# Attention and two expert layers on one core: all three token-block pairs as seven block products

## The chip, the cores and the metric

The kernel runs on one core of a Trainium2 chip. Its time is the device time of one execution in microseconds (us); what is quoted is the median of three runs. An execution with the profiler on is read beside them. TensorE does the matrix products (PE in the profile, its weight loads PEld), VectorE (DVE), ScalarE (ACT) and GpSimd (POOL) the rest, SyncE (SP) starts most transfers. SBUF is the on-chip memory, PSUM the eight banks that TensorE writes.

## The reference

Three layers follow one another; each needs the whole output of the one before, token by token.

```python
def phi(x):                                   # linear attention, 4 batches x 8 heads x 576 tokens x 64
    proj = einsum('bhsd,df->bhsf', x, w_phi)  # 128 features
    proj = proj - max(abs(proj), axis=-1)
    return concatenate([exp(proj), exp(-proj)], axis=-1)
kv, z = einsum('bhsf,bhsd->bhfd', phi(k), v), sum(phi(k), axis=2)
attn = einsum('bhsf,bhfd->bhsd', phi(q), kv) / (einsum('bhsf,bhf->bhs', phi(q), z) + 1e-06)
# dense gated layer on x = attn as 2304 tokens x 512, hidden width 1536
g, val = x @ w_gate, x @ w_val
x2 = (g * sigmoid(g) * val) @ w_out
# routed layer: 8 experts, each token to the one with the largest logit
e = argmax(x2 @ w_gate2)
out = prob[e] * sigmoid(x2 @ w_output_gate)[e] * (relu(x2 @ w1[e]) @ w2[e])
```

The dense layer's weights arrive as 64-bit floating point numbers, all else as 32-bit ones.

## The kernel before

**Attention** goes in 16 units: one batch and two heads each. A unit has three chunks of `qk_mm` (TensorE), `qk_sub` (VectorE: a reduction and a subtraction over 768 numbers per partition) and `k_exp` (ScalarE), then `kv_mm`, the transposes of the query features `tq_mm` with their exponentials, `num_mm` in two halves, `normalise` (VectorE: three instructions) and the transposes `tx_mm`, whose result is cut into a high and a low part (`x_hi`, `x_lo`). Four units give the 512 features of the 576 tokens of one batch.

**Cutting in two.** A product of 32-bit accuracy is made of three faster ones: the operands are cut into a high part (a rounded copy, on ScalarE) and a low part (the rest, by a subtraction on VectorE or GpSimd), and TensorE adds high x high, high x low and low x high in PSUM. So every 128x128 piece of a weight costs three matmuls.

**Weight conversion.** 36 weight pieces of 128x512 are loaded as 64-bit numbers into three staging buffers and turned into 32-bit ones with integer arithmetic: `conv_scale` (ScalarE), `conv_round` (ScalarE or GpSimd), `conv_bits` (VectorE, two instructions) and `conv_add` (GpSimd).

**The dense layer** goes over six blocks of 384 tokens and, in each, over 12 slices of 128 hidden features. In blocks 0 to 3 a slice takes 12 matmuls for the gate, 12 for the value (`gv_mm`, 384 columns) and 9 for the output (`o_mm`, 512 columns), and its three weight pieces are cut anew in each block. Blocks 4 and 5 go together (`pair`): gate and value of both blocks form a 2x2 block product, computed with seven products instead of eight (Strassen's scheme in Winograd's form), each of 6 matmuls. That takes sums of the weights (`pair_split`, GpSimd) and of the operands (`x_sums`, VectorE). Block 4's output product runs along. The hidden values of block 5 are kept in place of weights that are done with, and a stretch behind the pair multiplies them by the output weights, 9 matmuls a slice.

**After a dense block** its output is copied and stored (`post_x2`), and small instructions turn it, make the logits and route the tokens (`post_log`, `post_mm`, `post_sum`, `route_a`, `route_b`).

**Order.** The attention of units 0 to 7, the conversion and block 0 are issued in the order of a table, `PLAN_TABLE`; `Plan.run` goes through it and puts `warmup` matmuls on TensorE where its own bookkeeping has a gap. Units 8 to 15 are spread over blocks 1 to 3 by `pace`. Each engine takes its instructions strictly in its own order, and so does SP with its transfers. Behind the dense layer comes the routed one (`quads`, `moe2`), fed by gathers from the stored rows `x2d`.

Of the kernel before, what the change touches and what calls it, by code (L numbers as in the profile page):

```python
# [19 lines left out]
P = 128  # L20
# [14 lines left out]
NSG = 25  # L35
BIG = float(1 << 20)
# [18 lines left out]
class Arena:  # L55
# [12 lines left out]
PLAN_TABLE = [0, 4, 2, 1, 13, 14, 5, 3, 16, 15, 30, 17, 19, 31, 22, 20, 11, 32, 18, 6, 7, 12, 46, 33, 34, 47, 21, 23,  # L68
# [30 lines left out]

class Plan:  # L100

    LAT = 20
    SINGLES = (7, 0, 3, 5, 1, 2, 6)
    PAIRS = (5, 0, 2, 1, 6)  # L110
# [1425 lines left out]
```

## Time and profile before

| | us |
|---|---|
| median of three runs | 886.86 (886.61 to 888.32) |
| profiled execution: its time | 885.83 |
| profiled execution: span, first to last instruction | 884.1 |
| TensorE busy | 864.3 (98%) |
| VectorE, ScalarE, GpSimd busy | 526.7, 474.6, 386.1 |

The span is what the profile shows between the first and the last instruction; 1.7 us of the execution lie around it. A matmul's listed duration runs from its start to its modelled end, and the next one starts before that; what a matmul costs in a full row is the distance between starts. Five places divide the span: 66.9 us (first matmul of the dense layer), 170 us (about the end of the planned part), 485.6 us (first block product of blocks 4-5), 604.7 us (start of the stretch behind them) and 636.7 us (the routed layer).

### The profile page before, as it was taken

How to read it: one execution, taken by the hardware profiler on the slowest of the kernel's cores; microseconds unless marked ns; L12 is line 12 of the kernel's file. 1: busy time of each engine (PE TensorE's matmuls, PEld its weight loads, DVE VectorE, ACT ScalarE, POOL GpSimd, SP SyncE). 2: the span in 40 equal slices, each digit the busy share in tenths (PEclk: the TensorE clock that was granted, in tenths of full speed). 3: DMA queues.
4: the chain of work that ended last, by engine and by line, in shares of the span. 5: the costliest groups of instructions: out<-in, count | busy, mean ns of one | idle time of the engine just before them, and what ended most of it. 6: DMA issues, size and time to landing. Idle time of an engine off the chain costs nothing. (4 is left out here: it accounts for less than half of the span.)

```text
span 884.1 us, 17277 instructions
## 1 busy us (share of the span) xinstructions
PE 864.3 (98%) x6846; PEld 752.7 (85%) x6848; DVE 526.7 (60%) x1028; ACT 474.6 (54%) x921; POOL 386.1 (44%) x339
## 2 busy tenths in 40 slices
PE   8989999999999999999999999999999999999995
PEld 5779989889998998888899999998778888888784
DVE  6999786543434645346647676676676444345693
ACT  5867876544444444453456655565433434344783
POOL 1676989445453434343446666546401112120120
PEclk9999999999999999999999999999999999999998
DMA  8766544110011111020000000005901233010650
GB/s 240 220 188 205 167 143 138 45 36 1 1 31 49 44 43 28 17 78 2 1 2 0 36 1 1 1 1 202 343 6 39 104 105 136 23 50 1 237 209 11
DMA packets 20362, 70.41 MB, mean 80 GB/s; under 512 B 5294, under 2 KB 5550, under 8 KB 18992
## 3 DMA queue, kind: packets, MB, share of 16 engines
q1 hardware_dynamic: 16704, 59.21, 20.7%
q0 software_dynamic: 3200, 9.48, 3.3%
q8 instruction: 55, 0.90, 0.4%
q10 hardware_dynamic: 368, 0.53, 0.2%
q14 instruction: 35, 0.29, 0.1%
HBM read 72.84 MB, written 10.00 MB: 94 GB/s over the span
## 5 line engine op out<-in xcount | busy, mean ns | idle before, releaser
L529 POOL TENSOR_TENSOR arena_r<-arena,arena_r 128x512 fp32r<-128x512 f32 x143 | 183.9, 1290 | 176.2 <-ACT arena_r L525 172.6
L525 ACT ACTIVATE arena_r<-arena 128x512 fp32r<-128x512 f32 x143 | 90.1, 631 | 156.8 <-PE banks L546 97.0
L545 PE MATMUL banks<-arena_r 128*128 128x384 f32 x384 | 135.0, 352 | 0.0
L547 PE MATMUL banks<-arena_r 128*128 128x384 f32 x384 | 129.2, 336 | 0.0
L546 PE MATMUL banks<-arena_r 128*128 128x384 f32 x384 | 129.2, 336 | 0.0
L1209 ACT ACTIVATE arena_r<-arena 128x512 fp32r<-128x512 f32 x64 | 40.2, 632 | 100.7 <-PE banks L1220 49.7
L1212 DVE TENSOR_TENSOR arena_r<-arena,arena_r 128x512 fp32r<-128x512 f32 x64 | 44.2, 694 | 83.6 <-ACT arena_r L1209 81.3
L582 PE MATMUL banks<-arena_r 128*128 128x512 f32 x216 | 87.7, 407 | 0.0
L584 PE MATMUL banks<-arena_r 128*128 128x512 f32 x216 | 85.2, 394 | 0.0
L583 PE MATMUL banks<-arena_r 128*128 128x512 f32 x216 | 85.0, 393 | 0.0
L545 PEld LDWEIGHTS banks<-arena_r 128*128 128x128 f32 x384 | 72.1, 188 | 5.0 <-issue 1.3
L642 ACT ACTIVATE arena_r<-arena 128x512 fp32r<-128x512 f32 (+1 forms) x73 | 43.8, 612 | 54.2 <-PE banks L677 35.1
L546 PEld LDWEIGHTS banks<-arena_r 128*128 128x128 f32 x384 | 72.3, 188 | 0.6
L547 PEld LDWEIGHTS banks<-arena_r 128*128 128x128 f32 x384 | 72.1, 188 | 0.1
L1170 POOL DMA_INDIRECT out_dram<-arena x20 | 23.9, 1194 | 108.8 <-ACT arena L1264 39.1
L557 DVE SCALAR_TENSOR_TENSOR arena<-arena,banks 128x384 f32<-128x384 f32 x48 | 26.4, 551 | 67.4 <-ACT arena L554 67.4
L324 DVE TENSOR_REDUCE arena<-banks 128x6 f32<-128x768 f32 x48 | 45.8, 954 | 31.1 <-PE banks L316 30.2
L1165 POOL DMA_INDIRECT ov_gather<-x2d,arena x20 | 20.4, 1022 | 98.6 <-PE banks L1179 60.0
L643 POOL TENSOR_TENSOR arena_r<-arena,arena_r 128x512 fp32r<-128x512 f32 x37 | 48.1, 1299 | 29.9 <-ACT arena_r L642 28.9
L316 PEld LDWEIGHTS banks<-arena 64*128 64x128 f32 x576 | 38.3, 187 | 16.8 <-issue 9.7
L1219 PE MATMUL banks<-arena_r 128*128 128x512 f32 x128 | 50.2, 393 | 0.8 <-ACT arena_r L1209 0.8
L1233 PE MATMUL banks<-arena_r 128*128 128x512 f32 x128 | 51.0, 398 | 0.0
(165 smaller groups left out, 2084.8 us busy)
## 6 DMA issues: line engine op xcount, KB each, us to landing
arena<-mw SPq DMA_DIRECT2D x16, 2048.0 KB
ov_conv<-w1cat SPq DMA_DIRECT2D x24, 512.0 KB
arena<-w1cat SPq DMA_DIRECT2D x12, 512.0 KB
arena<-v SPq DMA_DIRECT2D x16, 325.0 KB
x2d<-arena SPq DMA_DIRECT2D x18, 256.0 KB
arena<-qT SPq DMA_DIRECT2D x15, 288.0 KB
arena<-kT SPq DMA_DIRECT2D x15, 288.0 KB
ov_gather<-x2d,arena POOLq DMA_INDIRECT x20, 3.4
```

The source lines that it names most:

```text
L324: DVE.tensor_reduce(out=MX, in_=ps, axis=AX.X, op=ALU.max, apply_absolute_value=True)
L525: ACT.activation(WH[i % 4], WR[f][w], AF.Copy)
L529: POOL.tensor_tensor(out=WL[i % 4], in0=WR[f][w], in1=WH[i % 4].bitcast(F32), op=ALU.subtract)
L545: PE.matmul(ps, wh[:, c], xh, start=(k == 0), stop=False)
L546: PE.matmul(ps, wh[:, c], xl, start=False, stop=False)
L547: state["pe"] = PE.matmul(ps, wl[:, c], xh, start=False, stop=(k == 3)).ins
L582: PE.matmul(ps, gh[:, ts_], woh, start=(f == 0), stop=False)
L583: PE.matmul(ps, gh[:, ts_], wol, start=False, stop=False)
L584: mm = PE.matmul(ps, gl[:, ts_], woh, start=False, stop=(f == NFT - 1))
L643: eng.tensor_tensor(out=w[1], in0=src, in1=w[0].bitcast(F32), op=ALU.subtract)
L1219: PE.matmul(ps, wh[:, c], XQH[:, k, :], start=(k == 0), stop=False)
L1233: PE.matmul(ps, h[:, c], wh, start=(f == 0), stop=False)
```

## The change

All 16 attention units and all 36 conversions now come first, in the order of a new table, with no dense block beside them. Then the three pairs of blocks 0-1, 2-3 and 4-5 each run as `pair` and a stretch, `down`, behind it. `gv_mm`, `o_mm`, `pace` and the steps of units 8 to 15 are gone.

Of the new parts: the 36 sign bits are made on GpSimd (`conv_sign`), which leaves VectorE one instruction of two in `conv_bits`. The exponentials of a unit's keys are two instructions over 1152 numbers instead of six over 384. Both feature buffers have two copies for all units; the second lies in memory that the dense layer takes over afterwards (`second`). Attention output for blocks 2 to 5 is stored to memory in 28 pieces (`x_keep`, `x_store`) and read back, a pair ahead, as `XF`. The operand sums of blocks 0-1 are made on TensorE by 44 matmuls with plus or minus the identity (`sum_mm`); those of the later pairs on VectorE and ScalarE in the stretch before (`x_sums2`, 7 steps). In the first two pairs the second block's hidden values are stored to memory (`hd`) and eight slices of twelve are read back in the stretch: the places that the last pair uses for them, those of the gate weights, are still needed by the next pair.

```diff
-PLAN_TABLE = [0, 4, 2, 1, 13, 14, 5, 3, 16, 15, 30, 17, 19, 31, 22, 20, 11, 32, 18, 6, 7, 12, 46, 33, 34, 47, 21, 23,
+PLAN_TABLE = [
+    0, 1, 2, 3, 5, 542, 13, 14, 549, 15, 16, 4, 6, 28, 543, 17, 20, 30, 18, 546, 44, 46, 29, 7, 21, 19, 32, 45, 22, 33,
...
+    def k_exp(u):
+        kq = KQ[two(u)]
+        t = kq[:, :, 0:P]
+        ACT.activation(kq[:, :, P:2 * P], t, AF.Exp, scale=-1.0)
+        ACT.activation(t, t, AF.Exp)
...
+    def x_keep(u, piece, b, i):
+        c, j, o, w = piece
+        ACT.activation(XS[i][:, 0:w], PS[:, b, c:c + w], AF.Copy)
+
+    def x_store(u, piece, i):
+        c, j, o, w = piece
+        SP.dma_start(out=xd[j][:, u % 4, o:o + w], in_=XS[i][:, 0:w])
...
+    def conv_sign(i):
+        hi = ST[i % 3].rearrange("p (n two) -> p n two", two=2)[:, :, 1]
+        POOL.tensor_scalar(out=WR[i // 3][i % 3].bitcast(I32), in0=hi, scalar1=0.0, scalar2=-2.0 ** 31, op0=ALU.is_lt, op1=ALU.mult)
+
     def conv_bits(i, b):
-        ui, ai, wi = PS[:, b, :].bitcast(I32), CA.bitcast(I32), WR[i // 3][i % 3].bitcast(I32)
-        DVE.tensor_scalar(out=ai, in0=ui, scalar1=-2 ** 31, scalar2=None, op0=ALU.bitwise_and)
-        DVE.scalar_tensor_tensor(out=wi, in0=ui, scalar=3, in1=ai, op0=ALU.logical_shift_left, op1=ALU.bitwise_or)
+        ui, wi = PS[:, b, :].bitcast(I32), WR[i // 3][i % 3].bitcast(I32)
+        DVE.scalar_tensor_tensor(out=wi, in0=ui, scalar=3, in1=wi, op0=ALU.logical_shift_left, op1=ALU.bitwise_or)
...
+    SUMS = dict(S1=("+01", "-00"), S2=("+11", "-01", "+00"), A22=("+10", "-11", "+01", "-00"), S3=("+11", "-01"))
+
+    def sum_mm(name, b):
+        for k in range(2):
+            out_ = PS[:, b + k, :BT]
+            n = 2 * len(SUMS[name])
+            for i, t in enumerate(SUMS[name]):
+                for h in range(2):
+                    PE.matmul(out_, ident_r["+-".index(t[0])], XHL[int(t[1]), int(t[2])][h][:, k, :],
+                              start=(i + h == 0), stop=(2 * i + h == n - 1))
...
+    def fin(d, hl):
+        ACT.activation(hl[0], d, AF.Copy)
+        DVE.tensor_tensor(out=hl[1], in0=d, in1=hl[0].bitcast(F32), op=ALU.subtract)
+
+    def x_sums2(p):
...
+        def less(d, x, y, hl):
+            DVE.tensor_tensor(out=d, in0=x, in1=y, op=ALU.subtract)
+            fin(d, hl)
+
+        return [(fin, b21, opx["A12"]), (fin, b11, opx["A11"]), (less, sb_, b22, b12, opx["S3"]),
+                (less, sb_, b12, b11, opx["S1"]), (less, sb_, b22, sb_, opx["S2"]), (fin, b22, opx["S4"]),
+                (less, sb_, b21, sb_, opx["A22"])]
...
         def o_part(f, ts):
-            n, g = (4, f - 1) if f else (3, NFT - 1)
-            o_tiles(n, g, ts, OUTB, (GH[g % 2], GL[g % 2]), W2)
+            g = (f - 1) % NFT
+            if f:
+                o_tiles(g != 0, g == NFT - 1, ts, bk["O"], (GH[g % 2], GL[g % 2]), W2)
...
+            add(hb(p, f), gb, pa, ALU.mult)
+            if p < NP - 1:
+                SP.dma_start(out=hd[p][f], in_=hb(p, f))
...
+    def down(p):
+        fine(1000)
...
+        for i, f in enumerate(order_):
+            if i >= 2:
+                cut(g5(p, i), hb(p, f), DVE)
+            w = slot(48 * p + 36 + i)
+            cut(w, WR[f][2], POOL)
+            if not end and i >= 2 and i < 10:
+                SP.dma_start(out=HS3[order_[i + 2] % 4], in_=hd[p][order_[i + 2]])
+            mm = o_tiles(i > 0, i == NFT - 1, range(3), bk["O2"], g5(p, i), w)
...
+            if i >= 2:
+                fill(1)
+            if not end:
+                if i >= 3 and xs:
+                    x = xs.pop(0)
+                    x[0](*x[1:])
+                if i == 7:
+                    cut22(0)
+                if 8 <= i < 11:
+                    pair_split(48 * p + 40 + i)
...
+    for p in range(NP):
+        state["banks"] = BANKS[p]["free"]
+        pair(p, rest)
+        down(p)
```

**How the order moves.** On TensorE, before, these rows lead from the attention of the planned part to the first gate matmuls (L545 to L547). L316 is `qk_mm`, L426 `tx_mm`, L407 `num_mm`, L387 `tq_mm`, L365 the larger part of `kv_mm`.

```order
L365 MATMUL banks<-arena 64x65 x32
L316 MATMUL banks<-arena 128x128 x6
L426 MATMUL banks<-arena 128x128 x5
L407 MATMUL banks<-arena 64x65 x20
L387 MATMUL banks<-arena 128x128 x3
L407 MATMUL banks<-arena 64x65 x20
L387 MATMUL banks<-arena 128x128 x3
L316 MATMUL banks<-arena 128x128 x6
L426 MATMUL banks<-arena 128x128 x5
L545 MATMUL banks<-arena_r 128x384
L546 MATMUL banks<-arena_r 128x384
L547 MATMUL banks<-arena_r 128x384
```

On TensorE, now, these are the last rows of the attention and the first block product (L583, L584). L396 is `num_mm`, L357 and L366 `kv_mm`, L381 `tq_mm`, L410 `tx_mm`, L515 `sum_mm`; `arena,r_att` is the second copy of the buffers (unit 14), `arena` the first (unit 15).

```order
L396 MATMUL banks<-arena,r_att 64x65 x40
L357 MATMUL banks<-arena 64x130 x4
L366 MATMUL banks<-arena 64x65 x32
L381 MATMUL banks<-arena 128x128 x3
L410 MATMUL banks<-arena 128x128 x5
L396 MATMUL banks<-arena 64x65 x40
L515 MATMUL banks<-arena_r,arena_r_63 128x384 x20
L410 MATMUL banks<-arena 128x128 x3
L515 MATMUL banks<-arena_r,arena_r_63 128x384 x24
L410 MATMUL banks<-arena 128x128 x2
L583 MATMUL banks<-arena_r,r_dense 128x384
L584 MATMUL banks<-arena_r,r_dense 128x384
```

What moved: dense work used to start after about six units and to stand between the rest; now it starts behind all sixteen, and between the last attention chunk of `qk_mm` and the first product TensorE has units 14 and 15 to finish and the 44 sums to make.

On GpSimd, before, in the planned part: L502 is `conv_round`, L513 `conv_add`, L529 the low parts of block 0's weights.

```order
L502 TENSOR_SCALAR ov_conv<-arena 128x512
L513 TENSOR_TENSOR arena<-arena 128x512
L529 TENSOR_TENSOR arena_r<-arena,arena_r 128x512
L502 TENSOR_SCALAR arena<-ov_conv 128x512
L513 TENSOR_TENSOR arena<-arena,ov_conv 128x512
L502 TENSOR_SCALAR ov_conv<-ov_conv 128x512
L513 TENSOR_TENSOR arena<-arena 128x512
```

On GpSimd, now, in the middle of the first stage: L455 is `conv_round`, L461 `conv_sign`, L469 `conv_add`.

```order
L455 TENSOR_SCALAR arena<-ov_conv 128x512
L461 TENSOR_SCALAR arena<-arena 128x512
L461 TENSOR_SCALAR arena<-ov_conv 128x512
L469 TENSOR_TENSOR arena<-arena,ov_conv 128x512
L469 TENSOR_TENSOR arena<-arena 128x512
L461 TENSOR_SCALAR arena<-ov_conv 128x512
L469 TENSOR_TENSOR arena<-arena 128x512
```

What moved: the cutting of block 0's weights left this place, and 36 sign instructions came in, one ahead of each piece's `conv_bits` on VectorE.

On VectorE, before, in the stretch behind blocks 4-5: L643 is the low part of the hidden values, L921 to L936 the routing's copies of block 4.

```order
L1407 MEMSET ov_gather 128x516 x4
L643 TENSOR_TENSOR arena_r<-arena,arena_r 128x384 x2
L921 COPY arena<-banks 128x512
L643 TENSOR_TENSOR arena_r<-arena,arena_r 128x384
L921 COPY arena<-banks 128x512
L643 TENSOR_TENSOR arena_r<-arena,arena_r 128x384
L921 COPY arena<-banks 128x512
L643 TENSOR_TENSOR arena_r<-arena,arena_r 128x384
L930 COPY arena<-banks 128x384
L936 COPY arena<-banks 128x48
```

On VectorE, now, in the stretch behind blocks 0-1: L542 is the low part of the hidden values, L838 the routing's copy, L534 and L524 the two kinds of instruction in the operand sums (a difference, a low part).

```order
L524 TENSOR_TENSOR arena_r<-arena,arena_r 128x768
L534 TENSOR_TENSOR banks<-arena 128x2x384
L542 TENSOR_TENSOR r_dense<-arena,r_dense 128x384
L524 TENSOR_TENSOR arena_r<-banks,arena_r 128x768
L838 COPY arena<-banks 128x512
L542 TENSOR_TENSOR r_dense<-arena,r_dense 128x384
L534 TENSOR_TENSOR banks<-arena 128x2x384
L542 TENSOR_TENSOR r_dense<-arena,r_dense 128x384
L838 COPY arena<-banks 128x512
L524 TENSOR_TENSOR ov_pair<-banks,ov_pair 128x768
L534 TENSOR_TENSOR banks<-arena,banks 128x2x384
L838 COPY arena<-banks 128x512
```

What moved: the operand sums of the next pair, 11 instructions of 768 numbers, came in between the low parts of the hidden values that each slice's 9 matmuls wait for.

## Rows read from the trace of the kernel before

**Rows 1.** Stretches: us, busy us (instructions) by engine, clock, DMA share, GB/s.
```profile
0.00:66.90 66.90, 59.48 (x1070) 48.22 (x1072) 57.08 (x96) 46.90 (x101) 33.63 (x33) 1.00 0.74 214
66.90:170.00 103.10, 103.10 (x997) 94.32 (x996) 77.63 (x138) 73.05 (x148) 83.20 (x65) 1.00 0.46 141
170.00:485.60 315.60, 315.60 (x2858) 282.44 (x2857) 155.90 (x319) 153.94 (x322) 143.94 (x117) 1.00 0.09 26
485.60:604.70 119.10, 118.49 (x650) 109.53 (x649) 81.85 (x171) 66.91 (x138) 68.88 (x76) 1.00 0.02 8
604.70:636.70 32.00, 32.00 (x172) 25.61 (x172) 21.29 (x59) 15.63 (x31) 19.41 (x17) 1.00 0.89 340
636.70:884.10 247.40, 235.67 (x1110) 192.63 (x1107) 133.00 (x249) 118.21 (x184) 36.98 (x33) 0.99 0.25 87
```

**Rows 2.** Timeline, TensorE, blocks 4-5: start, us, instruction; two unbroken runs.
```profile
564.50 0.33 PE L677 MATMUL banks<-arena_r 128*128 128x384 f32 x1
...
568.32 0.34 PE L678 MATMUL banks<-arena_r 128*128 128x384 f32 x1
...
607.25 0.39 PE L583 MATMUL banks<-arena_r 128*128 128x512 f32 x1
...
612.91 0.39 PE L584 MATMUL banks<-arena_r 128*128 128x512 f32 x1
```

**Rows 3.** Timeline, TensorE, attention beside nothing else: start, us, instruction.
```profile
26.96 0.44 PE L426 MATMUL banks<-arena 128*128 128x128 f32 x2
27.23 0.49 PE L387 MATMUL banks<-arena 128*128 128x128 f32 x3
27.56 0.49 PE L426 MATMUL banks<-arena 128*128 128x128 f32 x3
27.98 2.55 PE L407 MATMUL banks<-arena 128*64 128x65 f32 x80
30.47 0.55 PE L387 MATMUL banks<-arena 128*128 128x128 f32 x3
30.94 0.94 PE L316 MATMUL banks<-arena 64*128 64x128 f32 x12
31.81 0.66 PE L356 MATMUL banks<-arena 128*64 128x130 f32 x8
32.30 2.04 PE L365 MATMUL banks<-arena 128*64 128x65 f32 x64
```

**Rows 4.** One line's instructions: ns min/median/max, first and last start.
```profile
L316 PE MATMUL banks<-arena x576: 272/272/373, 5.4 to 436.0; 64*128 64x128 f32 x192
```

**Rows 5.** Groups by line on VectorE: busy us, mean ns, idle before.
```profile
L327 DVE TENSOR_TENSOR arena<-banks,arena 128x768 f32<-128x768 f32 x48 | 45.9, 957 | 1.6
L324 DVE TENSOR_REDUCE arena<-banks 128x6 f32<-128x768 f32 x48 | 45.8, 954 | 31.1 <-PE banks L316 30.2
...
L509 DVE SCALAR_TENSOR_TENSOR arena<-banks,arena 128x512 int32<-128x512 int32 x36 | 24.9, 691 | 1.2
...
L421 DVE TENSOR_TENSOR arena<-banks,arena 128x320 f32<-128x320 f32 x32 | 15.7, 490 | 1.1
L444 DVE TENSOR_TENSOR arena_r<-banks,arena_r 128x192 fp32r<-128x192 f32 x32 | 10.4, 349 | 3.1 <-ACT arena_r L440 3.1
...
L420 DVE RECIPROCAL arena<-arena 128x5 f32<-128x5 f32 x32 | 6.1, 191 | 1.1
...
L419 DVE TENSOR_SCALAR arena<-banks 128x5 f32<-128x5 f32 x32 | 5.0, 157 | 4.3 <-PE banks L407 4.3
```

**Rows 6.** Weight conversion on GpSimd: one line, one group.
```profile
L502 POOL TENSOR_SCALAR arena<-arena x4: 1519/1532/1552, 16.5 to 131.7; 128x512 int32<-128x512 uint32 x4
...
L513 POOL TENSOR_TENSOR arena<-arena 128x512 int32<-128x512 int32 x27 | 34.7, 1289 | 19.6 <-DVE arena L509 13.5 <-DVE arena L419 4.6 <-ACT arena_r L440 1.1
```

**Rows 7.** VectorE, low parts: both inputs in SBUF, and one in PSUM.
```profile
L643 DVE TENSOR_TENSOR arena_r<-arena,arena_r x36: 494/691/1818, 482.2 to 632.1; 128x512 fp32r<-128x512 f32 x24, 128x384 fp32r<-128x384 f32 x12
...
L632 DVE TENSOR_TENSOR arena_r<-banks,arena_r x2: 958/958/958, 477.0 to 483.5; 128x768 fp32r<-128x768 f32 x2
```

More of the change, by code (lines that the diff above doesn't have):

```diff
@@ L35 @@
 NSG = 25
+NP = NBLK // 2
 BIG = float(1 << 20)
@@ L281, in bank_no @@
         used[b] = state["n"]
-        return b
-    def pair_no():
-        state["n"] += 1
-        b = min((b for b in state["banks"] if b + 1 in state["banks"]),
-                key=lambda x: (max(used[x], used[x + 1]), min(used[x], used[x + 1])))
-        used[b] = used[b + 1] = state["n"]
         return b
@@ L308, in two @@
     def two(u):
-        return u % 2 if u < PROL else 0
+        return (u + 1) % 2
     def qk_mm(u, c, b):
@@ L375, in kv_copy @@
             eng.tensor_copy(KV[u % 2], ps)
-    def step_kv(u):
-        b = bank_no()
-        kv_mm(u, b)
-        kv_copy(u, b)
     def qp(u):
-        return QP[two(u)] if u < QSW else QP[2]
+        return QP[two(u)]
     def tq_mm(u, c, b):
@@ L408, in num_mm @@
                               stop=(a == 1), skip_group_check=True)
-    def step_num(u):
-        for h in range(2):
-            b = bank_no()
-            num_mm(u, h, b)
-            normalise(h, b)
     def normalise(h, b):
@@ L432, in x_pieces @@
             w = min(n, BT - o)
-            out.append((c0 - 384 * part, j % 3, o, w))
+            out.append((c0 - 384 * part, j, o, w))
             c0 += w
@@ L436, in x_pieces, with x_hi, x_lo @@
         return out
-    def x_hi(u, part, b):
-        for c, j, o, w in x_pieces(u, part):
-            ACT.activation(XH[:, j, u % 4, o:o + w], PS[:, b, c:c + w], AF.Copy)
-    def x_lo(u, part, b):
-        for c, j, o, w in x_pieces(u, part):
-            DVE.tensor_tensor(out=XL[:, j, u % 4, o:o + w], in0=PS[:, b, c:c + w],
-                              in1=XH[:, j, u % 4, o:o + w].bitcast(F32), op=ALU.subtract)
-    def step_tx(u, part):
-        b = bank_no()
-        tx_mm(u, part, b)
-        x_hi(u, part, b)
-        x_lo(u, part, b)
-    steps, mark = [], {}
-    def add(f, *a):
-        steps.append((f, a))
-    def qk(u):
-        return [(step_qk, u, c) for c in range(3)] if u < 16 else []
+    def x_keep(u, piece, b, i):
[4 more added lines that the diff above has]
+        SP.dma_start(out=xd[j][:, u % 4, o:o + w], in_=XS[i][:, 0:w])
+    def x_hi(u, piece, b):
+        c, j, o, w = piece
+        ACT.activation(XH[:, j, u % 4, o:o + w], PS[:, b, c:c + w], AF.Copy)
+    def x_lo(u, piece, b):
+        c, j, o, w = piece
+        DVE.tensor_tensor(out=XL[:, j, u % 4, o:o + w], in0=PS[:, b, c:c + w],
+                          in1=XH[:, j, u % 4, o:o + w].bitcast(F32), op=ALU.subtract)
     def warmup(n):
@@ L641, in cut, with cut_lo, weight_sum @@
+    def cut_lo(w, src, eng):
+        eng.tensor_tensor(out=w[1], in0=src, in1=w[0].bitcast(F32), op=ALU.subtract)
     def cut(w, src, eng):
         ACT.activation(w[0], src, AF.Copy)
[L643 removed]
+        cut_lo(w, src, eng)
+    def weight_sum(f, i):
+        g0, g1 = WR[f][0][:, 0:256], WR[f][0][:, 256:512]
+        v0, v1 = WR[f][1][:, 0:256], WR[f][1][:, 256:512]
+        s1, s2, s3, s4 = SS[f % 2]
+        o, x, y, op = ((s1, v0, v1, ALU.add), (s2, s1, g0, ALU.subtract), (s3, g0, v0, ALU.subtract),
+                       (s4, g1, s2, ALU.subtract))[i]
+        POOL.tensor_tensor(out=o, in0=x, in1=y, op=op)
@@ L664, with product @@
     PLACE = {"A11": (0, 0), "A12": (0, 1), "S1": (1, 0), "S2": (1, 1), "S3": (2, 0), "S4": (2, 1)}
-    def product(f, name, bank_, start):
+    def product(p, f, name, bank_, start):
         if name == "A22":
@@ L682, in cut22, with hb, g5, stretch @@
             cut(opx["w22"], WR[f][1][:, 256:512], POOL)
-    def h5(f):
-        if f < NFT:
-            cut(G5(f), HB5[f], DVE)
-    def G5(f):
-        if f < 2:
-            return XH[:, 1, f, :], XL[:, 1, f, :]
-        return GH[f % 2], GL[f % 2]
-    def pair(rest):
+    def hb(p, f):
+        return HB5[f] if p == NP - 1 else HS3[f % 4]
+    def g5(p, i):
+        if i < 2:
+            return XH[:, 2, i, :], XL[:, 2, i, :]
+        return GH[i % 2], GL[i % 2]
+    def stretch(p):
+        return list(range(NFT)) if p == NP - 1 else [8, 9, 10, 11] + list(range(8))
+    def pair(p, rest):
         def add(out_, x, y, op=ALU.add):
@@ L748, in pair @@
             cut(W2, WR[f][2], POOL)
-            rest(f, 2)
+            rest(p, f, 2)
             if f == NFT - 1:
-                h5(0)
-                h5(1)
+                for i in range(2):
+                    cut(g5(p, i), hb(p, stretch(p)[i]), DVE)
         hidden(NFT - 1)
@@ L859, in filler @@
+        op("ACT", 42, lambda: ACT.activation(opx["w22"][0], WR[0][1][:, 256:512], AF.Copy), [("wr", 1), ("ovp",)], [("h22",)], due=d)
+        op("POOL", 75, lambda: cut_lo(opx["w22"], WR[0][1][:, 256:512], POOL), [("h22",), ("wr", 1)] + [("sum", n) for n in SUMS],
+           [("l22",), ("ident_r",)], due=d)
         def filler(eng, t0, t1):
@@ L1360 @@
     first_part()
-    state["banks"] = [5, 6, 7]
-    need = {1: mark[8] - 2, 2: mark[12] - 2, 3: mark[15]}
-    prev = (0, NFT - 1)
+    last_places()
     def post(n):
@@ L1474, with rest @@
-    gather_q(1)
-    for i in range(3):
-        post_x2(5, i)
+    todo = []
+    def rest(p, f, g):
+        if f == 0:
+            if g != 2:
+                return
+            if p:
+                for i in range(3):
+                    post_x2(2 * p - 1, i)
+                if p == NP - 1:
+                    todo.extend(route_early() + [(slot_map, (EARLY_T, 4 * NEQ, 0, True))])
+                todo.extend(post(2 * p - 1))
+            if p < NP - 1:
+                for j in range(2):
+                    SP.dma_start(out=XF[j], in_=xd[2 * p + 2 + j])
+        fine(2)
@@ new lines, in down @@
+    def down(p):
+        fine(1000)
+        bk, n, end = BANKS[p], 2 * p + 1, p == NP - 1
+        state["banks"] = bk["down"]
+        todo.extend(post(n - 1))
+        xs = [] if end else x_sums2(p)
+        if end:
+            load_w(0, 0)
+        order_ = stretch(p)
+        for i, f in enumerate(order_):
[6 more added lines that the diff above has]
+            mm = o_tiles(i > 0, i == NFT - 1, range(3), bk["O2"], g5(p, i), w)
+            if end or i == 8:
+                state["pe"] = mm.ins
+            if end and 2 <= i < 6:
+                gather_q(0, [i - 2])
+            if i == 1:
+                o_tiles(True, True, range(3), bk["O"], (GH[1], GL[1]), W2)
+                for t in range(3):
+                    post_x2(n - 1, t)
+                if end:
+                    load_w(0, 1)
+                    rows()
+            if i >= 2:
[8 more added lines that the diff above has]
+                    pair_split(48 * p + 40 + i)
+            elif i >= 8:
+                xt_q(0, i - 8)
+        if end:
+            gather_q(1)
+            for i in range(3):
+                post_x2(n, i)
```

478 lines of the change are left out of this document (163 added, 315 removed), and 66 rows, old and new, of the table PLAN_TABLE.

## The prediction, made before the changed kernel ran

> **What bounds the kernel now.** I read the stretches first, then the timeline of TensorE, then the groups of VectorE and GpSimd. The stretches show one bound nearly everywhere [rows 1]: TensorE is busy 103.1 of 103.1 us, 315.6 of 315.6 us and 118.5 of 119.1 us in the dense part, at a granted clock of 1.00, which is the upper of its two levels. Only the first 66.9 us are another's: there VectorE has 57.1 us of work, and as the first attention matmul starts at 5.4 us [rows 4] and VectorE about a microsecond later, that is 57.1 of 60.5 us, or 94%. TensorE idles 7.4 us of that stretch, 12% of what is left after 5.4 us. So the change is a trade between two places. In the dense part every matmul less is time saved. In the attention part, dense matmuls used to fill whatever the other engines left open, and that filling goes.
>
> A matmul costs the distance between two starts in a full row [rows 2]: 23 starts of 384 columns from 564.50 to 568.32 make 22 steps of 0.1736 us, and 26 starts of 512 columns from 607.25 to 612.91 make 25 steps of 0.226 us. (Listed durations are twice that, because they overlap.)
>
> **A first sum over matmuls.** Blocks 0 to 3 have 4 x 12 x 24 = 1152 gate and value matmuls; two pairs have 2 x 12 x 42 = 1008. That is 144 x 0.1736 = 25.0 us less. The sums of blocks 0-1 add 44 x 0.1736 = 7.6 us. If nothing else moved, the gain were 17.4 us, and the time 869. What else moves is worked out by stages: first stage T1 (start to first block product), three pairs with their stretches T2, the routed layer T3.
>
> **T1, from TensorE's side.** One unit's work by starts [rows 3]: three chunks `qk_mm` of 0.87 (30.94 to 31.81) = 2.61; `kv_mm` 0.49 + 2.04 = 2.53; three `tq_mm` of 0.33 to 0.47, taken as 0.42, = 1.26; both halves of `num_mm` 2.49; `tx_mm` 0.27 + 0.42 = 0.69. Together 9.58, times 16 = 153.3 us. With the start at 5.4, the sums at 7.6 and seven `warmup` matmuls that the new order leaves inside the stage (7 x 0.226 = 1.6) this is 167.9 us without a gap. That is the lower end. The upper end takes the idle share of the first 66.9 us: (167.9 - 5.4) / 0.88 + 5.4 = 190 us.
>
> **T1, from VectorE's side** [rows 5]. 48 chunks x (0.957 + 0.954) = 91.7; 32 halves of `normalise` x (0.157 + 0.191 + 0.490) = 26.8; 36 `conv_bits`, now one instruction, x 0.691 = 24.9; the low parts of blocks 0-1, eight of 192 columns at 0.349 and four of 384 at no more than twice that, 5.6. Together 149.0 us. The order puts five `conv_bits` and four halves of `normalise` (6.9) behind the last chunk, so 142.1 stand before its end. At the 94% of the old first stage that end comes at 6.4 + 142.1/0.94 = 157.6. Behind the last `qk_mm`, 1.9 us earlier, TensorE still has units 14 and 15 and the sums: two `kv_mm` (5.1), two and a half `num_mm` (6.2), `tx_mm` for two units and a piece (1.7), three `tq_mm` (1.3), 44 sums (7.6) = 21.8 us. So T1 = 157.6 - 1.9 + 21.8 = 177.5. I take **177**; it lies 9 above TensorE's own sum, about 4 of which are the first unit's way through VectorE, during which TensorE has nothing else.
>
> ScalarE loses nothing here: its exponentials become fewer and longer. GpSimd gets the 36 sign instructions. The trace has no such instruction; the nearest rows are the strided rounding at 1.53 us and the plain addition at 1.29 us [rows 6]. I take 1.53, as it also reads every second number. Then GpSimd has 36 x (1.53 + 1.29) + 24 roundings x 1.53 = 138 us from its first conversion at about 16.5 on, and is done near 155: hidden behind the 157.6 above, with little to spare. Transfers carry the same attention and weight bytes as before at 214 GB/s and a share of 0.74 in the first stretch; 28 stores of attention output are added. Their wait stands on SP, in one queue with the loads; a late store holds `x_keep` on ScalarE, as there are two buffers. I cost it at nothing, as the transfers of the first stretch had room at that share, and count a late store under the loose first stage below.
>
> **T2.** The old pair and its stretch took 119.1 + 32.0 = 151.1 us [rows 1]. In them 504 x 0.1736 = 87.5 are products and 225 x 0.226 = 50.9 output matmuls; 12.7 are the work after blocks 3 and 4, the early routing, four turned tiles and gaps. The last pair loses the 9 matmuls that block 3 left it (2.0): 149.1. The middle pair has no early routing and no turned tiles; the first has also only one block behind it. Their rest lies between 0 and 12.7; I take 10.5 and 6.5, so 87.5 + 48.9 + 10.5 = 146.9 and 142.9. Together 438.9.
>
> To this come the operand sums in the two middle stretches. VectorE had 21.3 us of work in the old stretch of 32.0 [rows 1]. Eleven instructions of 768 numbers at 0.958 [rows 7] and two weights' low parts at 0.691 add 11.9; what falls away (the clearing and the turned tiles of the gather) I leave in, so 33.2 at most, against some 29 of TensorE. Four of the seven steps also make VectorE wait for ScalarE's copy between their two instructions, and the low part that the next 9 matmuls need is queued behind. Nothing says it must cost anything, since the sums begin before the pair ends; at worst it is the excess, 4, and some 6 of such waits, so 0 to 10 each. I take 4 each, **8** in all.
>
> The row of low parts with both inputs in SBUF runs from 0.494 to 1.818 us [rows 7], three times and more, while those with one input in PSUM stay at 0.958. The Trainium skill (SBUF — State Buffer, "Who interferes with whom") says that a VectorE instruction with two SBUF inputs blocks against a GpSimd instruction that reads SBUF, the later one for the other's whole length. The trace agrees. Five of the eleven new instructions are of that kind; by the rule each may wait a GpSimd instruction of 1.29 us, 6.5 us a stretch, and the total would come out up to 5 us higher than with my 8.
>
> The spills of hidden values (24 stores, 16 loads) go through SP beside TensorE; each load is issued two slices, or 4 us, ahead. I cost them at nothing; without that cover a slice waits the missing part of a load, which I count within the 0 to 10.
>
> **T3** keeps its 247.4 us: the same instructions at other addresses.
>
> **Sum.** 177 + 438.9 + 8 + 247.4 = 871.3 of span, against 884.1. Around the span lay 1.7 us, and the median is 1.0 above the profiled execution: 874.0.
>
> **The rivals.**
> - *The first stage runs near its floor.* Two copies of both buffers and eight free banks speak for it, 94% busy VectorE in the old stage against it. T1 168 to 172 and free stretches: 857 to 866.
> - *The stretches are VectorE's.* 10 us each instead of 4: 886, no change. For it: 33.2 us of work and the blocked low parts [rows 7]; against it: the sums are spread over seven slices.
> - *The first stage is as loose as the old one was for TensorE.* All four engines are near full now, each in its own order, and one late instruction stops the next engine; no dense matmul covers it. T1 = 190 to 200: 887 to 897. Against it: VectorE's work per unit fell, as half of `conv_bits` left.
> - *Signs cost more than GpSimd has (slower).* GpSimd then sets T1: 16.5 + 36 x 1.29 + 24 x 1.53 = 99.6, plus 36 times the sign's length. T1 may be 189.8 before the gain is gone (886.9 - 2.7 - 247.4 - 438.9 - 8), so this decides from 2.5 us a sign on. At two passes of 1.53 it is 210, and the time 907. Against it: no listed GpSimd instruction of this width exceeds 1.55 us.
>
> **Chances.** Forecast (866 to 883) 0.58; near the floor 0.14; stretches VectorE's (883 to 888) 0.09; loose first stage 0.13; signs 0.06. Range 860 to 891: left out are the lower half of the second case and the upper part of the last two. A measurement of this kernel can tell 0.2%, or 1.8 us, from no change. Faster by more: 0.58 + 0.14 + 0.03 = 0.75; within: 0.07; slower by more: 0.18.
>
> **What would show it.** First block product at 172 to 182 us; VectorE's last 768-wide reduction near 156 to 158; GpSimd's signs at 1.3 to 1.55 us; TensorE 100% busy in the three pairs, each 110 to 117 us long; gaps of 2 to 6 us, released by VectorE, in the two middle stretches; the routed layer again about 247 us. A first product after 190 us, or middle stretches of more than 40 us, make the forecast wrong.

## The result, and the profile after

The changed kernel takes 873.4 us (median; 872.6 to 878.5 over four runs) against 886.7 for the kernel before in the same comparison: a ratio of 0.986, 95% interval 0.982 to 0.990. In the experiments, on another occasion, it measured 872.6 against 886.05, 0.9853 (0.9838 to 0.9868). The forecast was 874.0 us. The profiled execution took 872.99 us, with a span of 871.2; forecast for the span: 871.3.

The stretches of the changed kernel (columns as in [rows 1]): the first stage up to the first block product, the three pairs each with its stretch, and the routed layer.

```profile
0.00:177.30 177.30, 163.02 (x3292) 145.59 (x3293) 146.52 (x248) 125.55 (x240) 160.20 (x115) 1.00 0.74 216
177.30:325.30 148.00, 143.57 (x756) 129.84 (x755) 94.77 (x173) 85.80 (x171) 95.97 (x102) 1.00 0.15 49
325.30:474.00 148.70, 146.44 (x786) 132.05 (x785) 101.25 (x199) 86.40 (x174) 91.92 (x97) 1.00 0.12 38
474.00:624.10 150.10, 148.45 (x811) 133.36 (x810) 99.39 (x227) 81.27 (x166) 86.57 (x91) 1.00 0.21 78
624.10:871.20 247.10, 235.70 (x1109) 192.62 (x1107) 133.01 (x249) 117.93 (x184) 34.64 (x33) 0.99 0.25 87
```

TensorE's busy time over the six rows of [rows 1] is 864.3 us, over these five 837.2: 27.2 less. The prediction's first sum counts 17.4 us of matmuls; where the other 9.8 lie, no run takes apart. Its idle time went from 19.8 to 34.0 us, 14.3 more, and 12.9 us of span are left. So the change did what it set out to do on TensorE and paid half of it back in idle time. The question for the experiments is who makes TensorE idle, first of all in the first stage: the fifth busy figure of the first row is GpSimd's, 160.2 of 177.3 us, nearly TensorE's own.

GpSimd in the first stage, answering to [rows 6]: first the instructions of single lines (ns min/median/max, first and last start), L461 the sign and L455 the rounding, then the group of L469, the addition (busy us, mean ns, idle before).

```profile
L461 POOL TENSOR_SCALAR arena<-ov_conv x24: 1957/1980/2014, 10.6 to 167.6; 128x512 int32<-128x512 f32 x24
L461 POOL TENSOR_SCALAR arena<-arena x12: 1946/1982/2019, 21.2 to 173.0; 128x512 int32<-128x512 f32 x12
...
L455 POOL TENSOR_SCALAR arena<-ov_conv x12: 1534/1550/1987, 12.6 to 171.0; 128x512 int32<-128x512 uint32 x12
```

```profile
L469 POOL TENSOR_TENSOR arena<-arena 128x512 int32<-128x512 int32 x24 | 30.5, 1277 | 0.5
```

A sign takes 1.98 us, not the 1.53 of the nearest row before. Rounding and addition cost what they cost before. From its first sign at 10.6 us to the end of the stage GpSimd is busy 158.6 of 166.7 us.

VectorE's groups in the same stage, answering to [rows 5], and the instructions of two lines, of which the first answers to [rows 4]:

```profile
L335 DVE TENSOR_REDUCE arena<-banks 128x6 f32<-128x768 f32 x48 | 45.8, 954 | 13.1 <-PE banks L329 11.2
L465 DVE SCALAR_TENSOR_TENSOR arena<-banks,arena 128x512 int32<-128x512 int32 x36 | 24.1, 682 | 8.8 <-POOL arena L461 6.1 <-ACT arena L386 2.7
```

```profile
L329 PE MATMUL banks<-arena x576: 272/272/373, 4.9 to 151.5; 64*128 64x128 f32 x192
...
L335 DVE TENSOR_REDUCE arena<-banks x48: 946/958/960, 6.1 to 154.0; 128x6 f32<-128x768 f32 x48
```

The second row shows one way in which GpSimd reaches TensorE: `conv_bits` (L465) now waits for a sign, 6.1 us in all, and the attention work queued behind it on VectorE waits with it. The chain of waits, pieces in order of time (start us, us, what), says the same; from 60 us to the end of the stage most of its time reads like these pieces. (A weight load of 9.1 us from 95.8 on and two stores of attention output from 137.5 on, 9.2 us together, are in it too.)

```profile
72.78 1.24 POOL arena L469
74.02 0.08 issue
74.10 1.54 POOL arena L455
75.72 3.93 POOL arena L461 x2
...
165.73 3.89 POOL arena L461 x2
169.62 1.27 POOL arena L469
170.96 1.99 POOL arena L455
...
188.69 1.23 POOL r_dense L542
189.97 0.45 PE banks L585
```

The last two lie behind the first block product: pair 0 still waits for a weight's low part that stood behind late conversions in GpSimd's queue.

A second way runs through the staging buffers. TensorE's longest stop in the stage, 2.67 us, ends at 162.0 and is released by `conv_scale` (L448) on ScalarE, which had waited for a weight load itself. SP had held back the loads of the last pieces (L445) until GpSimd was done with a buffer. The first line is from TensorE's timeline, the second from SP's waits between 150 and 161.5 us.

```profile
162.02 0.66 PE L357 MATMUL banks<-arena 128*64 128x130 f32 x8 [2.67 <-ACT banks L448]
...
SPq L445 <- POOL arena L461: 6.3, 2, 3.6
```

TensorE's waits between 177.3 and 624 us (line, waited for: us in total, times, longest), then the gaps at the starts of the three stretches in its timeline:

```profile
PE banks L478 <- DVE arena_r L542: 3.4, 3, 1.3
PE banks L585 <- POOL r_dense L542: 1.5, 1, 1.5
PE banks L793 <- DVE arena L793: 1.0, 1, 1.0
PE banks L845 <- DVE arena L838: 0.6, 1, 0.6
...
PE banks L478 <- DVE r_dense L542: 0.5, 1, 0.5
```

```profile
294.51 0.96 PE L478 MATMUL banks<-r_dense,arena_r 128*128 128x512 f32 x3 [0.88 <-DVE arena_r L542]
...
443.83 0.96 PE L478 MATMUL banks<-r_dense,arena_r 128*128 128x512 f32 x3 [1.28 <-DVE arena_r L542]
...
593.12 0.73 PE L478 MATMUL banks<-r_dense,arena_r 128*128 128x512 f32 x2 [1.27 <-DVE arena_r L542]
```

L542 on `arena_r` is the low part of the first hidden slices that a stretch multiplies. The third gap has the size of the second, and the third stretch has no operand sums.

### The profile page after: what moved, and what is told of

It is laid out like the page before. It is cut to its first block, busy times and chain, and to the rows that moved or that the text cites. A ratio compares the mean times of both kernels' runs of the same rounds, so it can differ in the third digit from the quotient of the medians.

```text
span 871.2 us, 17442 instructions
## 1 busy us (share of the span) xinstructions
PE 837.2 (96%) x6746; PEld 733.5 (84%) x6746; DVE 574.9 (66%) x1095; ACT 496.9 (57%) x932; POOL 469.3 (54%) x435
## 4 chain that ended last, share of the span: by engine, by line
PE 68%; POOL 12%; DVE 8%; issue 5%; DMA 4%; ACT 2%; POOLq 0%; DVEq 0%; ACTq 0%
PE banks L583 10%; PE banks L584 9%; PE banks L585 9%; PE banks L478 5%; PE banks L476 5%; PE banks L477 5%; POOL arena L461 5%; POOL arena L469 3%; PE banks L1138 3%; PE banks L1154 3%; PE banks L1139 3%; PE banks L1153 3%; PE banks L1152 3%; PE banks L1140 3%; POOL arena L455 2%
## 5 line engine op out<-in xcount | busy, mean ns | idle before, releaser
L545 ACT ACTIVATE r_dense<-arena 128x512 fp32r<-128x512 f32 (+1 forms) x171 | 102.5, 611 | 136.2 <-PE banks L584 107.4
L554 POOL TENSOR_TENSOR arena<-arena 128x256 f32<-128x256 f32 x144 | 105.8, 747 | 98.7 <-DVE r_dense L542 95.8
L542 POOL TENSOR_TENSOR r_dense<-arena,r_dense 128x512 fp32r<-128x512 f32 x72 | 94.8, 1318 | 64.1 <-ACT r_dense L545 61.4
L542 DVE TENSOR_TENSOR r_dense<-arena,r_dense 128x512 fp32r<-128x512 f32 (+1 forms) x102 | 70.9, 697 | 52.7 <-ACT r_dense L545 52.6
L1128 ACT ACTIVATE arena_r<-arena 128x512 fp32r<-128x512 f32 x64 | 40.3, 633 | 104.9 <-PE banks L1139 49.8
L585 PE MATMUL banks<-arena_r,r_dense 128*128 128x384 f32 x288 | 96.8, 336 | 1.5 <-POOL r_dense L542 1.5
L583 PE MATMUL banks<-arena_r,r_dense 128*128 128x384 f32 x288 | 96.5, 340 | 0.6 <-DVE arena L605 0.4
L584 PE MATMUL banks<-arena_r,r_dense 128*128 128x384 f32 x288 | 96.8, 336 | 0.0
L605 DVE TENSOR_TENSOR banks<-arena,banks 128x384 f32<-128x384 f32 x144 | 79.9, 555 | 12.7 <-PE banks L585 9.5
L583 PEld LDWEIGHTS banks<-arena_r,r_dense 128*128 128x128 f32 x288 | 54.0, 188 | 4.9 <-ACT arena L608 1.4
L584 PEld LDWEIGHTS banks<-arena_r,r_dense 128*128 128x128 f32 x288 | 54.1, 188 | 3.4 <-issue 0.6
L608 ACT ACTIVATE arena<-banks 128x384 f32<-128x384 f32 x108 | 51.9, 481 | 7.6 <-PE banks L585 6.7
L585 PEld LDWEIGHTS banks<-arena_r,r_dense 128*128 128x128 f32 x288 | 54.1, 188 | 2.4 <-POOL r_dense L542 1.8
L1138 PE MATMUL banks<-arena_r 128*128 128x512 f32 x128 | 50.2, 393 | 0.8 <-ACT arena_r L1128 0.8
L583 PE MATMUL banks<-ov_pair,r_dense 128*128 128x384 f32 x144 | 50.2, 348 | 0.4 <-ACT arena L608 0.3
L461 POOL TENSOR_SCALAR arena<-ov_conv 128x512 int32<-128x512 f32 x24 | 47.4, 1979 | 5.8 <-DMA ov_conv<-w1cat 5.3
L1139 PE MATMUL banks<-arena_r 128*128 128x512 f32 x128 | 50.0, 391 | 0.0
```

Source lines behind the costliest of these rows:

```text
L461: POOL.tensor_scalar(out=WR[i // 3][i % 3].bitcast(I32), in0=hi, scalar1=0.0, scalar2=-2.0 ** 31, op0=ALU.is_lt, op1=ALU.mult)
L542: eng.tensor_tensor(out=w[1], in0=src, in1=w[0].bitcast(F32), op=ALU.subtract)
L545: ACT.activation(w[0], src, AF.Copy)
L554: POOL.tensor_tensor(out=o, in0=x, in1=y, op=op)
L583: PE.matmul(ps, w[0][:, c], xh[:, k, :], start=(start and k == 0), stop=False, skip_group_check=True)
L584: PE.matmul(ps, w[0][:, c], xl[:, k, :], start=False, stop=False, skip_group_check=True)
```

## The experiments

Two theories for the first stage. **G**: GpSimd sets its end, through the signs. **V**: VectorE and TensorE's tail behind it set it, as the prediction had it, and GpSimd is hidden. Two for the stretches: **S**, the operand sums make VectorE late; **C**, the first cut of a stretch is late by itself.

**e1_control**, the changed kernel without an edit. 

> The changed kernel again, unedited, as the measure for the others. Time 873 us, first block product at 177.3 us.

Measured: 872.6 us, 0.9853 (0.9838 to 0.9868) of before, first block product at 176.9.

**e2_round_act**, GpSimd relieved:

```diff
-  alt=("POOL", 157, lambda i=i: conv_round(i, POOL)))
+  alt=("POOL", 157, lambda i=i: conv_round(i, ACT)))
```

> The 24 weight roundings that the order gives to GpSimd are issued on ScalarE, at the same places of the order. GpSimd loses 24 x 1.57 = 37.7 us of its 160.2 us in the first stage; ScalarE gets 24 x 0.69 = 16.6 us. Theory G (GpSimd sets the end of the first stage): the first block product falls from 177.3 to 168-172 us, TensorE's own sum, and the time to 864-868 us. Rival V (VectorE and TensorE's tail behind it set it, as the prediction had it): GpSimd was hidden, the first block product stays within 1 us of 177.3 and the time within 1 us of 873, or rises by what ScalarE's extra 16.6 us delay.

Measured: 865.3 us, 0.9769 (0.9756 to 0.9782). The first block product starts at 171.6. VectorE's `conv_bits` waits for signs only 2.5 us, and pair 0 waits no more for GpSimd. Its stretch up to the first product, and that group:

```profile
0.00:171.60 171.60, 163.18 (x3294) 145.58 (x3294) 145.99 (x248) 136.99 (x264) 125.71 (x94) 1.00 0.75 223
```

```profile
L465 DVE SCALAR_TENSOR_TENSOR arena<-banks,arena 128x512 int32<-128x512 int32 x36 | 24.1, 682 | 2.8 <-POOL arena L461 2.5
```

VectorE's 146 us are the same as in the changed kernel. With GpSimd at 125.7 instead of 160.2 us the stage ended 5.7 us earlier. TensorE's stop of 2.67 us at L357 is gone as well. V falls here; how much of the 5.7 us came by the signs and how much by the staging buffers, no run separates. This version beats both kernels.

**e3_sign_more**, GpSimd loaded:

```diff
+        for _ in range(2 if i % 4 == 1 else 1):
             POOL.tensor_scalar(... op0=ALU.is_lt, op1=ALU.mult)
```

> Nine of the 36 sign instructions (every fourth) are issued twice; the second writes the same values. GpSimd gets 9 x 1.98 = 17.8 us more. Theory G: the first block product comes up to 17.8 us later, at 190-195 us, and the time is 886-891 us. Rival V: GpSimd idles 17 us in this stage and has room: at most 2 us later, 873-875 us.

Measured: 888.9 us, 1.0033 (1.0021 to 1.0045): slower than the kernel before. First block product at 193.9, 16.6 us later than in the changed kernel, for 17.8 us of signs.

```profile
0.00:193.90 193.90, 173.10 (x3292) 153.31 (x3293) 147.53 (x248) 125.67 (x240) 177.50 (x124) 0.95 0.67 198
```

GpSimd has 177.5 us of work and idles 16.4; in the changed kernel it idled 17.1. Its additional work appears whole. The granted clock was 0.95 in this stage, so TensorE's own work is longer too (173.1 us busy). As GpSimd's idle time did not grow, I read the end of the stage as GpSimd's all the same, but this run does not separate it from the clock.

**e4_no_eps**, VectorE relieved:

```diff
-        DVE.tensor_scalar(out=den, in0=den, scalar1=1e-6, scalar2=None, op0=ALU.add)
```

> The 32 small VectorE instructions that add 1e-6 to the attention's denominators are left out (the quotients then lack that 1e-6). VectorE loses 32 x 0.163 = 5.2 us in the first stage. Theory G: the first block product stays at 177.3 within 1 us, time 872-873 us. Rival V: it comes 4 to 6 us earlier, at 171-173 us, time 867-869 us.

Measured: 873.6 us, 0.9862 (0.9847 to 0.9877), first block product at 178.4. Pair 0 does not wait for GpSimd here, so the stage and that wait end together where they did (178.4 against 177.3 + 1.5). Taking 5.2 us of work off VectorE gave nothing: G's figures are missed by 0.1 us of stage and 0.6 us of time, V's by 5.4 and 4.6. G holds.

**e5_sign_dve**, the sign back on VectorE, one part of the change undone:

```diff
-        POOL.tensor_scalar(out=WR..., in0=hi, ... op0=ALU.is_lt, op1=ALU.mult)
+        DVE.tensor_scalar(out=wi, in0=ui, scalar1=-2 ** 31, scalar2=None, op0=ALU.bitwise_and)
```

> The sign instructions go back to VectorE (a bitwise AND of the scaled weights, as in the kernel before, written where the sign goes), all 36; order otherwise as in the changed kernel. GpSimd loses 36 x 1.98 = 71.3 us, VectorE gets 36 x 0.69 = 24.8 us on top of its 146.5 us in the first stage. The prediction's way of costing VectorE (its work over 0.94, then TensorE's tail of 21.8 us) gives the first block product at 6.4 + (142.1 + 31 x 0.69)/0.94 - 1.9 + 21.8 = 200 us and 896 us. Theory G with VectorE loose: it has 171 us of work and fits, so the first block product comes at 172-180 us, time 866-875 us.

Measured: 881.2 us, 0.9934 (0.9920 to 0.9948), first block product at 187.8, between both numbers. Its stretch up to VectorE's last chunk, and the last reduction:

```profile
0.00:167.50 167.50, 150.25 (x2993) 129.76 (x2993) 152.95 (x252) 111.15 (x210) 80.70 (x72) 1.00 0.72 210
```

```profile
L335 DVE TENSOR_REDUCE arena<-banks x48: 947/948/960, 6.8 to 166.5; 128x6 f32<-128x768 f32 x48
```

Here I read VectorE as the bound: from 6.8 us to 167.5 it is busy 152.7 of 160.7 us, 95% (no run relieves it in this version). And 167.5 - 1.9 + 21.8 = 187.4: the prediction's formula for VectorE, share and tail, holds where VectorE is nearly full. What it got wrong is the work in front of that point: 163.5 us forecast, 152.7 measured. And the move of the sign is worth 7 to 9 us to the changed kernel, even at 1.98 us (7 by the ratios of the two occasions, 8.6 by their times).

**e6_sign_one**, the price of a sign:

```diff
-  scalar1=0.0, scalar2=-2.0 ** 31, op0=ALU.is_lt, op1=ALU.mult)
+  scalar1=0.0, scalar2=None, op0=ALU.is_lt)
```

> The sign instruction keeps its comparison and loses the multiplication by -2^31 (the converted weights then lack their signs, and the routing with them; only the first stage is read). If the second operation is what the sign costs over the rounding: 1.55 us each instead of 1.98, GpSimd loses 36 x 0.43 = 15.5 us, and by theory G the first block product comes at 171-173 us. If the price is that of reading every second 32-bit float, it stays at 1.98 us and at 177 us.

Measured, in a single execution: the second operation is the price.

```profile
L461 POOL TENSOR_SCALAR arena<-ov_conv x24: 1510/1546/1584, 10.7 to 163.1; 128x512 int32<-128x512 f32 x24
L461 POOL TENSOR_SCALAR arena<-arena x12: 1528/1545/2045, 21.4 to 167.5; 128x512 int32<-128x512 f32 x12
```

The first block product came at 173.3. So at the price that the prediction took, the first stage would have been 4.0 us shorter. But the last sign still starts at 167.5 us, while the prediction had GpSimd done near 155: behind its first sign GpSimd idles 18.3 of 162.7 us here.

**e7_no_sums**, the operand sums of the two middle stretches left out (`xs = []`), on top of e2. 

> With the roundings on ScalarE; and the operand sums of blocks 2-3 and 4-5 are left out of the two middle stretches (their products then use old operands, and the routing with them; only the two stretches are read). Theory S (the prediction's: VectorE is late there because of the sums): the gaps of 2.2 us in the first and 2.2 us in the second middle stretch go, 4 us in all. Rival C (the cut of the first hidden slice at the end of a pair is late by itself, as in the last stretch, which has no sums and has the same gap of 1.27 us): the gaps of 0.9 and 1.3 us behind the pair's end stay, and at most the 2.3 us of the small ones behind them go.

TensorE's waits in pairs and stretches, of this kernel and then of e2 (a single execution each; the small moves of routing work among the output matmuls that the scheduler makes with any edit are in both):

```profile
PE banks L478 <- DVE arena_r L542: 3.8, 3, 1.3
PE banks L583 <- DVE arena L605: 0.4, 1, 0.4
PE banks L583 <- ACT arena L608: 0.2, 1, 0.2
```

```profile
PE banks L478 <- DVE arena_r L542: 3.4, 3, 1.3
PE banks L793 <- DVE arena L793: 1.2, 2, 1.0
PE banks L845 <- DVE arena L838: 0.6, 1, 0.6
PE banks L478 <- DVE r_dense L542: 0.5, 1, 0.5
...
```

The gaps at the stretches' starts stay (3.8 us, three of 1.27). The small ones behind them, 1.2 + 0.6 + 0.5 = 2.3 us, go. C describes it; the sums cost at most 2.3 us of gaps in all. This kernel's time is not read, as its routed layer has other work.

**e8_early_cut**, on top of e2: the cut of each stretch's first hidden slice stands ahead of two additions:

```diff
+            if f == NFT - 1:
+                cut(g5(p, 0), hb(p, stretch(p)[0]), DVE)
             add(py, su2, py)
             add(py, GP, py, ALU.mult)
```

> With the roundings on ScalarE; and the cut of the first hidden slice of each stretch is issued right behind the last block product of the pair, ahead of two VectorE additions and the routing steps. Rival C: the gaps of 0.9, 1.3 and 1.3 us at the start of the three stretches go, the time falls from 865.3 to 861.5-862.5 us. Theory S: they move into the next low part, and the time stays at 865 within 1 us.

Measured: 866.3 us, 0.9775 (0.9757 to 0.9794), no different from e2. The waits show why:

```profile
PE banks L478 <- DVE r_dense L605: 2.2, 2, 1.1
...
PE banks L478 <- DVE arena_r L542: 0.5, 1, 0.5
...
```

The gaps of 3.4 us at L542 fell to 0.5, and 2.2 us came up at L605, the low part of the pair's last hidden slice, which the two additions now delayed. The time is what S had said of this run, though the sums are not the reason. C named the gap rightly and its remedy wrongly: at a pair's end VectorE owes TensorE two results, and the order only chooses which one is late.

**e9_more_xs**, on top of e2: four half buffers for the attention stores in place of two:

```diff
-    XS = [TS, GP]
+    XS = [TS[:, 0:192], TS[:, 192:384], GP[:, 0:192], GP[:, 192:384], TS, GP]
```

> With the roundings on ScalarE; and the two buffers from which attention output is stored are cut into halves of 192 columns, so that 24 of the 28 stores find four buffers instead of two. ScalarE's wait for a late store was 6.3 us in the changed kernel and is 4.5 us with the roundings on ScalarE; behind it VectorE waited 1.2 and TensorE 0.4 us. If that wait is on the path: first block product 1 to 2 us earlier (170 instead of 171.6), time 863-864.5 us. Rival (it is hidden behind TensorE's own work): the wait goes, and the first block product and the time stay within 0.5 us of 171.6 and 865.3.

Measured: 864.6 us, 0.9758 (0.9745 to 0.9771), not told from e2's 0.9769; first block product at 173.0. ScalarE's wait for stores went:

```profile
L424 ACT ACTIVATE arena<-banks 128x192 f32<-128x192 f32 (+1 forms) x28 | 9.6, 373 | 0.7 <-PE banks L410 0.7
```

It was 4.5 us in e2 and 6.3 in the changed kernel. No gain shows, as the rival says. But the first block product came 1.4 us later than in e2, outside the rival's 0.5, because TensorE had other pauses: those that no engine released (L366) went from 0.5 to 3.7 us. So a gain of a microsecond could hide here, and for the changed kernel, whose chain passes through two of these stores, the wait was not taken out.

**e10_act_no_eps**, e2 without the 1e-6. 

> With the roundings on ScalarE; and without the 32 small VectorE instructions that add 1e-6 to the denominators (5.2 us). If TensorE's own sum is what is left once GpSimd is relieved: first block product within 1 us of 171.6. If VectorE is the next bound: 167-169 us.

Measured, in a single execution: first block product at 172.3, VectorE 4.9 us less busy.

```profile
0.00:172.30 172.30, 162.87 (x3292) 145.59 (x3293) 141.11 (x216) 137.08 (x264) 125.38 (x94) 1.00 0.76 223
```

With GpSimd relieved, VectorE is not the bound either. What is left in e2 is TensorE's own work and 7.2 us of its pauses behind its start. Of them 3.2 lie before 17 us, on the first unit's way through VectorE and ScalarE. Whether the loads or GpSimd, busy 21.6 of the last 21.6 us, still hold back some of the others was not tested.

## Why the prediction was right, and where it was right by luck

**Total.** Forecast 871.3 us of span, measured 871.2. By stages: first stage 177 and 177.3; pairs with stretches 446.9 and 446.8; routed layer 247.4 and 247.1. The time was right to 0.1%. The reasons were right for TensorE's work in the pairs, and wrong or only near in the first stage; there the number is in part luck.

**TensorE's side of the first stage** was near. The sum was 167.9 us without a gap: 162.5 of work behind a start at 5.4. Measured are 159.3 us busy behind a start at 4.9, together 164.2. (The 163.0 of the row above also hold 3.7 us of `warmup` matmuls ahead of that start, so that 163.0 + 4.9 = 167.9 is a coincidence.) e2 comes within 7.4 us of it and stays there when VectorE (e10) is relieved. The prediction's 4 us for the first unit's way are 3.2 in the trace.

**The step that failed** is the GpSimd term: "I take 1.53 ... and is done near 155: hidden behind the 157.6 above, with little to spare". A sign took 1.98 us (36 x 0.45 = 16.2 us more). Weight sums and weights' low parts (lines L554 and L542, 5.7 and 3.8 us before the first product) were not in that sum. And GpSimd was taken to work without a pause, though each sign needs a staging buffer, which needs a load, and each addition needs VectorE's result: it paused 8.1 us behind its first sign, and 18.3 at the cheaper price, where the last sign still came at 167.5 (e6). The start was taken too late instead, which hid part of this: 16.5 us is the first rounding of one form in [rows 6], while the first sign stands at 10.6. So GpSimd was not hidden; it set the end of the stage. Relief from it gave 5.7 us of the stage and 1.5 us of pair 0, 7.3 us of time (e2).

**The VectorE path** gave 177.5 by errors that cancelled. Work in front of the last chunk's end: forecast 142.1 us, measured 134.4. Busy share up to there: forecast 94%, measured 90% (134.4 of the 149.8 us from 6.1 to 155.9), in part because `conv_bits` stood waiting for GpSimd. The last chunk ended at 155.9 against a forecast of 157.6. By the formula the stage would then end at 155.9 - 1.9 + 21.8 = 175.8; behind the last `qk_mm`, which ended at 151.8, TensorE had 22.0 us of work, as forecast, and 3.5 us of pauses, 2.67 of them the stop at L357. Had the sign cost what I took, the stage would have ended at 173.3 (e6) and the formula been 4 us too high. A measured number that agrees does not show that its path was the binding one; e2 and e4 did.

**The rivals.** "Signs cost more than GpSimd has" was the true mechanism at a smaller price. Its point of decision was well placed: forecast 2.5 us a sign. e3 is such a kernel, 45 signs in place of 36 or 2.48 us each on average, and it is 0.33% slower than before. Interpolated between e1 and e3, the gain is gone at about 2.4 us (an estimate; e3 also had the lower clock). But with 1.98 its sum gives only 99.6 + 36 x 1.98 = 170.9 us, 6.4 less than measured: the price alone would not have made GpSimd the bound, and the missing work and pauses are part of the cause. Its weight of 0.06 was too low: the argument against it ("no listed GpSimd instruction of this width exceeds 1.55 us") looked at instructions with one operation, and the sign has two. "The first stage runs near its floor" (857 to 866) is what e2 reaches at 865.3. A loose first stage and slow stretches did not come.

**Pairs and stretches.** TensorE's work in them was forecast as 438.9 us and is 438.5 (143.57 + 146.44 + 148.45). The gaps were forecast as 8 us and are 8.3. But they were to be the operand sums' in the two middle stretches, 4 us each. Measured: 2.0 and 2.2 us there, 1.3 in the last stretch, which has no sums, 1.5 in pair 0 from GpSimd, and the rest in pieces of at most 0.4 us. The sums themselves cost at most 2.3 us (e7). The mis-sized term is "4 each": it is about 1 each, and the rest of the 8 has other owners, so that this sum too came out by luck.

**Its other signs.** The first product and the routed layer came where forecast, and the gaps of the middle stretches at the lower edge of 2 to 6 us. Three missed: the signs took 1.98 us and not 1.3 to 1.55, VectorE's last reduction started at 154.0 and not near 156 to 158, and the pairs took 117, 118.5 and 119 us, the last two above the 110 to 117.

**The contention rule.** Low parts of the operand sums, both inputs in SBUF and then one in PSUM (L524, ns min/median/max), answering to [rows 7]:

```profile
L524 DVE TENSOR_TENSOR arena_r<-arena,arena_r x6: 954/1126/2006, 284.3 to 445.6; 128x768 fp32r<-128x768 f32 x6
L524 DVE TENSOR_TENSOR arena_r<-banks,arena_r x4: 948/952/958, 301.7 to 464.3; 128x768 fp32r<-128x768 f32 x4
```

The rule of the Trainium skill (SBUF — State Buffer, "Who interferes with whom") shows again: only the form with two SBUF inputs is stretched, up to 2.0 us. (That longest one started at 296.32 us, 0.10 us behind a GpSimd low part of 1.29 us.) Its price does not: with that result the total would have been up to 5 us higher, and leaving out the sums with all their stretching takes away at most 2.3 us of gaps. A stretched instruction costs TensorE only where it is the last one awaited.

**Costed at nothing:** the stores of attention output held ScalarE for 6.3 us; taking 4.5 us of that wait out of e2 gave no time (e9), and in the changed kernel it stays open. Rightly so costed, as far as the waits show: the spills of hidden values (no gap names them), ScalarE's longer exponentials, and the routed layer.

## What to carry to other kernels

An operation moved to an idle engine must be priced with its own number of operations, and the engine's whole queue, pauses for its inputs included, must be set against the stage: here 0.45 us times 36, 9.5 us of work that was not counted and the pauses together made an engine the bound that was to be hidden. When a forecast number comes true, take load off the engine you hold responsible and off its rival; only one of them moves the time. And after a kernel is tuned to one price list, look for the same work on the engine that does it cheapest: the rounding costs ScalarE 0.69 us and GpSimd 1.55.

## What was not expected of the hardware

A second operation in a GpSimd instruction is not free: 1.98 us against 1.546 for the same 128x512 numbers with the comparison alone (e6).

The granted clock fell in the first stage of some executions and not of others. In e3, stretches of 4 us show:

```profile
100.00:104.00 4.00, 2.13 (x69) 2.02 (x66) 3.48 (x7) 1.85 (x4) 3.92 (x3) 1.00 0.95 281
104.00:108.00 4.00, 3.40 (x19) 2.99 (x20) 1.32 (x2) 0.53 (x2) 3.92 (x4) 0.53 1.01 276
108.00:112.00 4.00, 4.00 (x58) 3.60 (x58) 1.71 (x5) 3.33 (x6) 3.70 (x3) 0.62 0.99 268
```

TensorE was idle 1.9 of the first 4 us, and then ran at 0.53 and 0.62, near the lower of its two levels (1.2 of 2.4 GHz), though busy for 3.4 and all of the next 4 us, before it was back at 1.00. Two more such falls came in this stage of e3, from 136 and from 172 us on. In e1, the changed kernel again, there was one:

```profile
156.00:160.00 4.00, 2.55 (x80) 2.36 (x79) 1.29 (x2) 3.19 (x7) 4.00 (x5) 1.00 0.44 136
160.00:164.00 4.00, 2.80 (x55) 2.83 (x57) 2.22 (x7) 0.61 (x1) 4.00 (x6) 0.73 0.56 156
164.00:168.00 4.00, 4.00 (x91) 3.71 (x90) 1.44 (x4) 3.60 (x10) 4.00 (x3) 0.84 0.32 81
```

e4 had one at the same place (0.58 from 164 us on); the other profiles of the series had none. In the first profile of the changed kernel the clock stayed at 1.00 there, with the same stop at L357 in front (2.67 us; 2.65 in e1) and TensorE busy 1.98 of the 4 us from 160 on. All these falls followed pauses of TensorE, but a pause of the same length did not always bring one. If it is the idle time that does it, which no run here isolates, a pause in a stage that another engine sets can cost TensorE more than its own length: the stage's TensorE work was 173.1 us in e3 and 164.8 in e1, against 163.0.
